# Fused cosformer attention and a GELU layer: the first chunk by halves of heads, and one batch's x turned a block earlier

## The chip, the cores and the metric

One core of a Trainium2 chip runs the whole kernel. The metric is the device time of one execution in microseconds (us), over three runs. A profiled execution of the same kernel gives the trace; its times count from the start of its span. The engines are called PE (matrix products), DVE (vector), ACT (scalar functions), POOL and SP; POOL and SP also issue most transfers (DMA).

## The reference

Eight batches, 8 heads, 576 positions, head size 64. `phi` is ReLU, weighted by a cosine and a sine of the position, so it has 128 features. The attention's result becomes `x` of 4608 tokens by 512, which goes through two matrix products with a GELU between them (2048 wide).

```
q_p = phi(q, cos_w, sin_w)                       # [B,H,S,128]
k_p = phi(k, cos_w, sin_w)
kv  = einsum('bhsf,bhsd->bhfd', k_p, v)          # 128 x 64 per head
z   = sum(k_p, axis=2)                           # 128 per head
num = einsum('bhsf,bhfd->bhsd', q_p, kv)
den = einsum('bhsf,bhf->bhs', q_p, z) + 1e-06
x   = (num / den), heads side by side            # [4608, 512]
h   = x @ w_in;  g = h * sigmoid(1.702 * h);  out = g @ w_out
```

## The kernel before, in words

The work goes batch by batch. The positions of a batch form four chunks of 128 and a tail of 64 (chunk 4). For each batch:

- `trig` (L135) or `trig_q` (L144) makes the weighted ReLU of q and k, in bf16, on DVE, ACT or POOL, two instructions for each `j` (64 positions a head pair).
- `kv_mm` (L202) sums `kv` on PE for pairs of heads `i`, with the row of `z` as a 65th column; `kv_evac` (L210) copies it into `kvs` on DVE. In batch 0 the v tile has no column of ones, and `ksum` (L214) makes `z` by itself, ahead of v's arrival.
- q has to lie features first: in batches 0 and 1 PE transposes it (`qturn_pe`, L167) into PSUM and `qevac` (L174) copies it to `qT` on DVE or ACT; from batch 2 on a DMA does (`qturn_dma`, L187).
- `num_mm` (L226) makes a chunk's numerators of eight heads, with the denominators as each head's 65th column, in a tile of two PSUM banks (four heads in each); `num_div` (L248) adds 1e-6 (`den`), inverts (`inv`) and divides (`xn`) on DVE. `den_early` (L241) makes the denominators by themselves, before the numerators are there.
- x has to lie features first too: in batches 0 and 1 `xturn_mm` (L269) transposes `xn` on PE into columns 264 to 391 of the same PSUM tile, beside the numerators, and `xturn_evac` (L276) copies that to `xT` on ACT; `xturn_dma` (L282) does it by DMA, for the tails in all batches.
- `mm1` (L303) multiplies by `w_in` in sixteen parts `fc` of 128 columns, each over four slices `kc` of 128 features, 512 tokens at a time; `mm1_part` (L291) does so for a range of tokens. `gelu` (L298) follows on ACT. `mm2` (L327) multiplies by `w_out` in ranges of `fc` for each group `t` of 128 tokens, an ACT copy takes the result to `ysb`, and a DMA writes it out. The 64-token tails of all batches go through together at the end.

PSUM has a pool of four one-bank tiles (`pmm`, L46), taken in turn by q's transposes, `den_early`, `mm1` and `mm2`, and a pool of two two-bank tiles (`pat`, L47) for `kv`, the numerators and batch 1's transposes of q. Each new tile waits until the last users of the one before it in that place are done.

The order on each engine is the order in the program; nothing is rescheduled. `idle` (L342) issues products of zeros on PE. At the start (L388 to L440), SP loads k and q of batch 0 in two pieces each, POOL loads v (converted to bf16), the first two parts of `w_in`, and later the rest.

`start_block` (L355) begins the `mm1` of a batch whose x is still being made: the first four `fc` run in parts of 128 tokens, a chunk at a time, between the numerators and the transposes of later chunks. Batches 0 and 1 begin so; batch 1 is called with `opened=True`, because its first two chunks are turned before, during batch 0's last `mm2` groups (L458 to L503). Batches 2 to 7 run all their `mm1` with 512 tokens at a time (L507 on), while q and x of the next batch are turned by DMA.

Of the kernel before, what the change touches and what calls it, by code (L numbers as in the profile page):

```python
# [9 lines left out]
F32 = mybir.dt.float32  # L10
BF16 = mybir.dt.bfloat16
# [8 lines left out]
def kernel(  # L20
# [9 lines left out]
    nc = tc.nc  # L30
# [67 lines left out]
    qn0 = qn.rearrange("p c h f -> p (c h f)")[:, 0:NS * NI * 128].rearrange(  # L98
        "p (j i f) -> p j i f", j=NS, i=NI)
    qT = one.tile([128, H, 640], BF16, name="qT")  # L100
    w_in_sb = [one.tile([128, KC, 512], BF16, name=f"w_in{g}") for g in range(4)]
    w_out_sb = one.tile([128, FC, d_model], BF16, name="w_out_sb")
    nc.gpsimd.memset(vt[:, :, :, 64:66], 1.0)
    nc.gpsimd.memset(qT[:, :, S:640], 0.0)
# [1 line left out]

    win_r = moe_w_in.rearrange("(kc p) f -> p kc f", p=128)
    wout_r = moe_w_out.rearrange("(g p c) d -> p g c d", p=128, c=4)
    w_in_v = [t.rearrange("p k (f c) -> p k c f", c=4) for t in w_in_sb]

    def w_in_of(kc, fc):
        return w_in_v[fc // 4][:, kc, fc % 4, :]

    def load(t, src, b, eng=nc.gpsimd):
        eng.dma_start(out=t, in_=src_of(src, b))
# [5 lines left out]
                            in_=q[b, :, 512:S, :].rearrange("h p d -> p h d"))  # L121

    def load_win(g):
        nc.gpsimd.dma_start(out=w_in_sb[g], in_=win_r[:, :, ts(g, 512)])

    def load_wout(g):
        nc.gpsimd.dma_start(out=w_out_sb[:, ts(g, 4), :], in_=wout_r[:, g])
# [46 lines left out]
    def qevac(c, act=False):  # L174
# [5 lines left out]
        else:  # L180
            nc.vector.tensor_copy(o, i)
# [41 lines left out]

    nums = {}

    def num_mm(c):  # L226
        ps = pat.tile([128, 2, 512], F32, name="at")
        for h in range(H):
            i, hh = divmod(h, 2)
            nc.tensor.matmul(ps[:, h // 4, ds((h % 4) * 65, 65)], qT[:, h, ts(c, 128)],  # L230
                             st["kvs"][:, hh, i, 0:65], start=True, stop=True)
        nums[c] = [ps]

    def inv_of(d):
        den = small.tile([128, 2, 4], F32, name="den")
# [3 lines left out]
        return inv  # L239

    def den_early(c):  # L241
        d = pmm.tile([128, 2, 4], F32, name="mm")
        for h in range(H):
            nc.tensor.matmul(d[:, h // 4, h % 4:h % 4 + 1], qT[:, h, ts(c, 128)],
                             st["kvs"][:, h % 2, h // 2, 64:65], start=True, stop=True)
        return inv_of(d)

    def num_div(c, inv=None):  # L248
        ps = nums[c][0]
        pv = ps[:, :, 0:260].rearrange("p a (h e) -> p a h e", h=4)  # L250
        if inv is None:
            inv = inv_of(pv[:, :, :, 64])
        xn = small.tile([128, 2, 4, 64], BF16, name="xn", bufs=4)
        nc.vector.tensor_tensor(xn, pv[:, :, :, 0:64],  # L254
                                inv.unsqueeze(3).to_broadcast([128, 2, 4, 64]), op=MUL)
        nums[c].append(xn)
# [9 lines left out]
    def x_of(b, c):  # L266
        return xt[:, :, ts(b, 64)] if c == 4 else x[b][:, :, ts(c, 128)]

    def xturn_mm(c):  # L269
        ps, xn = nums[c]  # L270
        xv = xn.rearrange("p a h e -> p (a h e)")
        for kc in range(KC):
            o = ps[:, kc // 2, ds(264 + (kc % 2) * 64, 64)].bitcast(BF16)
            nc.tensor.transpose(o, xv[:, ts(kc, 128)], ident)  # L274

    def xturn_evac(b, c):  # L276
        ps = nums.pop(c)[0]
        i = ps[:, :, 264:392].bitcast(BF16).rearrange("p a (k t) -> p a k t", k=2)
        o = x_of(b, c).rearrange("p (a k) t -> p a k t", a=2)
        nc.scalar.activation(o, i, AF.Copy)  # L280
# [7 lines left out]
    gT = {}  # L288
    hp = {}

    def mm1_part(b, fc, t0, t1):  # L291
        if t0 == 0:
            hp[fc] = pmm.tile([128, MT], F32, name="mm")
        for kc in range(KC):
            nc.tensor.matmul(hp[fc][:, t0:t1], w_in_of(kc, fc), x[b][:, kc, t0:t1],  # L295
                             start=(kc == 0), stop=(kc == KC - 1))
# [58 lines left out]
    def start_block(b, opened=False):  # L355

        if not opened:
            xturn_mm(0)
            xturn_evac(b, 0)
            num_mm(2)  # L360
            num_div(2)
            xturn_mm(1)
            xturn_evac(b, 1)
        def part(c, *fcs):
            for fc in fcs:
                mm1_part(b, fc, c * 128, c * 128 + 128)

        part(0, 0, 1, 2, 3)
        num_mm(3)
        num_div(3)  # L370
        xturn_mm(2)
        xturn_evac(b, 2)
        part(1, 0, 1, 2, 3)
        xturn_mm(3)
        xturn_evac(b, 3)
        num_mm(4)
        num_div(4)
        xturn_dma(b, 4)
        part(2, 0, 1, 2)
        part(3, 0, 1)  # L380
        part(2, 3)
        part(3, 2, 3)
        for fc in range(4):
            gelu(fc)
        mm1(b, 4)
# [25 lines left out]
    idle(2, w)
    qturn_pe(1)
    for j in (4, 5):
        trig(qn0, qf0, j)
    trig(qn0, qf0, 8, eng=nc.gpsimd)
    nc.gpsimd.tensor_copy(gate[0:1, 1:2], vb[0:1, 3, 0:1])
    load_win(2)
    load_win(3)
    kv_mm(0, 2, vb_rhs, 0, 64)
    qturn_pe(2)  # L420
    for j in (6, 7):
        trig(qn0, qf0, j, act=True)
    qevac(0)
    qevac(1)
    qevac(2, act=True)
    inv0 = den_early(0)
    kv_evac(0, 2, 64)
    kv_mm(2, 4, vb_rhs, 0, 64)
    kv_evac(2, 4, 64)
    qturn_pe(3)  # L430
    qevac(3, act=True)
    num_mm(0)
    num_div(0, inv0)
    num_mm(1)
    num_div(1)
    qturn_pe(4)
    qevac(4)
    idle(1)
    x_open(0)
    start_block(0)  # L440


    load(kf, k, 1)
# [15 lines left out]
        mm2(0, t, 0, 4)  # L459
    mm2(0, 0, 4, 8)  # L460
    mm2(0, 1, 4, 8)
    ha = at_homes()
    qturn_pe(0, ha[0])
    qturn_pe(1, ha[1])
    qevac(0)
    qevac(1, act=True)
    mm2(0, 2, 4, 8)
    mm2(0, 3, 4, 8)
    hb = at_homes()
    qturn_pe(2, hb[0])  # L470
    qturn_pe(3, hb[1])
    vcopy(0, 2)
    vcopy(2, 4, act=True)
    qevac(2)
    qevac(3, act=True)
    load_q(2, nc.gpsimd)
    load(kf, k, 2, nc.gpsimd)
    load(vf, v, 2, nc.gpsimd)
    mm2(0, 0, 8, 12)
    mm2(0, 1, 8, 12)  # L480
    hc = at_homes()
    qturn_pe(4, hc[0])
    qevac(4)
    kv_open()
    kv_mm(0, 4, vt_rhs, 0, 65)
    kv_evac(0, 4)
    mm2(0, 2, 8, 12)
    mm2(0, 3, 8, 12)
    num_mm(0)
    num_div(0)  # L490
    num_mm(1)
    num_div(1)
    x_open(1)
    mm2(0, 0, 12, 16)
    mm2(0, 1, 12, 16)
    xturn_mm(0)
    xturn_evac(1, 0)
    mm2(0, 2, 12, 16)
    xturn_mm(1)
    xturn_evac(1, 1)  # L500
    num_mm(2)
    num_div(2)
    mm2(0, 3, 12, 16)  # L503
    start_block(1, opened=True)


    for b in range(1, B):  # L507
        nb = b + 1 if b + 1 < B else None
        f0 = 5 if b == 1 else 0
        for fc in range(f0, FC):  # L510
            if nb is not None and fc == f0:
                for c in range(5):
                    trig_q(c)
                    qturn_dma(c)
                if nb + 1 < B:
                    load_q(nb + 1)
            if nb is not None and fc == f0 + 1:
                for j in range(NS if b > 1 else 5):
                    trig(kr, kf, j)
                vcopy(0, 4 if b > 1 else 2)  # L520
            mm1(b, fc)
            if b == 1 and fc in (7, 9, 11, 13):
                trig(kr, kf, (fc + 3) // 2, act=True)
        if b == 1:
            vcopy(2, 4, act=True)
        if nb is None:
            for fc in range(FC):
                mm1_tails(fc)
            for t in (4, 5, 6, 7):
                mm2(b, t, 0, FC)  # L530
            for t in range(3):
                mm2(b, t, 0, FC)
            mm2(b, 3, 0, FC, 0, 256)
            mm2(b, 3, 0, FC, 256, 512)
            continue
        x_open(nb)
        lag = 1 if b == 1 else 0
        for u in range(8):
            if u == lag:
                kv_open()  # L540
# [40 lines left out]
```

## Time and profile before

| | us |
|---|---|
| median of three runs | 292.51 (292.34 to 292.56) |
| the profiled execution | 292.51 |
| its span, first to last instruction | 290.8 |
| first `mm1` matmul of batch 0 | 16.20 |
| first `mm2` matmul of batch 0 | 31.38 |
| first `mm2` matmul of batch 1 | 65.11 |
| k of batch 0 lands (first, second piece) | 4.2, 6.1 |

A timeline row gives the start, the duration, the engine, the line, the operation with what it writes and reads, and in brackets the idle time of the engine ahead of it with what ended that. Rows of the same kind that follow each other are merged, and their number stands behind `x`. PE's matmuls are pipelined, so a matmul's own duration (0.19 us even for a small one) overlaps with the next one's: for what a matmul adds, look at the distance between starts. In the chain of the last work (shares of the span) PE has 92%, DMA 5%, DVE and POOL 1% each.

### The profile page before, as it was taken

Reading aid. Unit: us, or ns where it says so; the run is one execution under the profiler, and the core shown is the slowest. Engines: PE = TensorE matmul, PEld = TensorE weight load, DVE = VectorE, ACT = ScalarE, POOL = GpSimd, SP = SyncE. Lnnn points to the kernel's source line nnn. Section 1 sums busy time; section 2 is a strip of 40 time slices with the busy share of each in tenths; the row PEclk is TensorE's granted clock in tenths of the full one; section 3 lists DMA queues with packets and bytes.
Section 4 is the critical chain, followed back from the end, with each engine's and each line's share of the span. In section 5 each row is a group of like instructions: output and inputs, shape, how many; then the busy total and the mean of one; then the engine's idle time right before and its main releaser. Section 6 shows DMA issues by size and latency. Waiting matters only on the chain.

```text
span 290.8 us, 5789 instructions
## 1 busy us (share of the span) xinstructions
PE 284.3 (98%) x2330; PEld 154.8 (53%) x2330; DVE 124.1 (43%) x356; ACT 132.9 (46%) x232; POOL 37.8 (13%) x71
## 2 busy tenths in 40 slices
PE   7989999999999999999999999999999999999995
PEld 2775466755555554555455545554555455544444
DVE  4953645842648363826582567156624200000000
ACT  7957654693156214721463136412651167751111
POOL 6650044101210001001100110011000100002000
PEclk9999999999999999999999999999999999999999
DMA  7999999684689958975699469756975400002322
GB/s 250 244 214 287 372 267 363 172 181 128 126 225 306 220 132 276 260 197 145 225 277 227 122 192 335 184 143 152 379 94 74 117 36 3 0 0 44 87 88 72
DMA packets 67771, 52.48 MB, mean 180 GB/s; under 512 B 47969, under 2 KB 57953, under 8 KB 67745
## 3 DMA queue, kind: packets, MB, share of 16 engines
q1 hardware_dynamic: 60320, 32.52, 45.2%
q0 software_dynamic: 7424, 19.60, 23.6%
q8 instruction: 18, 0.29, 0.4%
q14 instruction: 9, 0.07, 0.1%
HBM read 36.70 MB, written 9.44 MB: 159 GB/s over the span
## 4 chain that ended last, share of the span: by engine, by line
PE 92%; DMA 5%; DVE 1%; POOL 1%; issue 0%; ACT 0%; ACTq 0%
PE mm L332 43%; PE mm L295 38%; PE mm L312 5%; DMA w_in<-in_moe_w_in_dram 3%; PE at L230 3%; PE at L207 3%; DMA kf<-in_k_dram 1%; PE at L171 1%; POOL vb L132 1%; DVE xn L254 0%; PE at L274 0%; DVE inv L238 0%; ACT ysb L336 0%; DVE den L236 0%; POOL gate L130 0%
## 5 line engine op out<-in xcount | busy, mean ns | idle before, releaser
L332 PE MATMUL mm<-w_out_sb,g 128*128 128x512 bf16 (+1 forms) x528 | 117.9, 373 | 0.0
L295 PE MATMUL mm<-xT,w_in 128*128 128x512 bf16 (+1 forms) x608 | 112.9, 345 | 0.2 <-DMA w_in<-in_moe_w_in_dram 0.2
L300 ACT ACTIVATE g<-mm 128x512 bf16<-128x512 f32 x128 | 75.1, 598 | 30.4 <-PE mm L295 30.2
L295 PEld LDWEIGHTS <-w_in 128*128 128x128 bf16 x608 | 61.6, 113 | 49.6 <-DMA w_in<-in_moe_w_in_dram 0.3
L332 PEld LDWEIGHTS <-g 128*128 128x128 bf16 x528 | 48.7, 97 | 49.6
L336 ACT ACTIVATE ysb<-mm 128x512 f32<-128x512 f32 (+1 forms) x37 | 21.7, 586 | 109.7 <-PE mm L332 106.7
L340 POOL DMA_DIRECT2D out_dram<-ysb x39 | 21.2, 547 | 205.6 <-ACT ysb L336 203.6
L142 DVE TENSOR_SCALAR kr<-kf,cosw 128x256 bf16<-128x256 f32 x64 | 22.5, 351 | 30.3 <-DMA kf<-in_k_dram 30.3
L254 DVE TENSOR_TENSOR xn<-at,inv 128x512 bf16<-128x512 f32 x40 | 27.7, 691 | 1.7 <-PE at L230 0.4
L142 DVE TENSOR_SCALAR kr<-kf,sinw 128x256 bf16<-128x256 f32 x64 | 22.6, 354 | 0.0
L236 DVE TENSOR_SCALAR den<-at 128x8 f32<-128x8 f32 x39 | 6.5, 166 | 34.4 <-PE at L230 34.4
L230 PEld LDWEIGHTS <-qT 128*128 128x128 bf16 x320 | 14.6, 97 | 8.1 <-issue 0.8
L212 DVE CAST kvs<-at 128x520 bf16<-128x520 f32 (+1 forms) x9 | 5.7, 635 | 28.9 <-PE at L207 28.9
L230 PE MATMUL at<-kvs,qT 128*128 128x65 bf16 x320 | 15.9, 193 | 0.7 <-ACT xT L280 0.7
L155 DVE TENSOR_SCALAR qn<-qf,sinw 128x512 bf16<-128x512 f32 (+1 forms) x30 | 14.4, 480 | 0.0
L155 DVE TENSOR_SCALAR qn<-qf,cosw 128x512 bf16<-128x512 f32 (+1 forms) x30 | 14.3, 476 | 0.0
L312 PE MATMUL mm<-xt,w_in 128*128 128x512 bf16 x64 | 14.0, 379 | 0.0
L332 PE MATMUL mm<-w_out_sb,gl_t 128*128 128x512 bf16 x64 | 14.0, 379 | 0.0
L313 ACT ACTIVATE gl_t<-mm 128x512 bf16<-128x512 f32 x16 | 9.6, 597 | 4.2 <-PE mm L312 4.2
L312 PEld LDWEIGHTS <-w_in 128*128 128x128 bf16 x64 | 7.2, 113 | 6.6
L207 PEld LDWEIGHTS <-kr 64*128 64x128 bf16 x576 | 9.3, 94 | 2.7 <-issue 2.5
L332 PEld LDWEIGHTS <-gl_t 128*128 128x128 bf16 x64 | 6.3, 98 | 7.5
(63 smaller groups left out, 115.4 us busy)
## 6 DMA issues: line engine op xcount, KB each, us to landing
kf<-in_k_dram SPq DMA_DIRECT2D x5, 1152.0 KB, 6.9
vf<-in_v_dram SPq DMA_DIRECT2D x5, 1152.0 KB, 9.6
qf<-in_q_dram SPq DMA_DIRECT2D x5, 1024.0 KB, 6.2
out_dram<-ysb POOLq DMA_DIRECT2D x20, 256.0 KB, 2.8
out_dram<-ysb POOLq DMA_DIRECT2D x19, 128.0 KB, 4.1
kf<-in_k_dram POOLq DMA_DIRECT2D x2, 1152.0 KB, 11.7
vf<-in_v_dram POOLq DMA_DIRECT2D x2, 1152.0 KB, 16.5
w_in<-in_moe_w_in_dram POOLq DMA_DIRECT2D x4, 512.0 KB, 10.2
```

Of the source, the lines that this page charges most:

```text
L142: eng.tensor_scalar(o, i, 0.0, w[:, j:j + 1], op0=MAX, op1=MUL)
L155: nc.vector.tensor_scalar(o, i, 0.0, sc, op0=MAX, op1=MUL)
L207: nc.tensor.matmul(st["kv", i][:, hh, ds(col, n)], kr[r, j, i, :], rhs(r, i, j), start=(j == 0), stop=(j == NS - 1))
L230: nc.tensor.matmul(ps[:, h // 4, ds((h % 4) * 65, 65)], qT[:, h, ts(c, 128)], st["kvs"][:, hh, i, 0:65], start=True, stop=True)
L254: nc.vector.tensor_tensor(xn, pv[:, :, :, 0:64], inv.unsqueeze(3).to_broadcast([128, 2, 4, 64]), op=MUL)
L295: nc.tensor.matmul(hp[fc][:, t0:t1], w_in_of(kc, fc), x[b][:, kc, t0:t1], start=(kc == 0), stop=(kc == KC - 1))
L300: nc.scalar.activation(g, hp.pop(fc), AF.Gelu_apprx_sigmoid)
L312: nc.tensor.matmul(hps, w_in_of(kc, fc), xt[:, kc, :], start=(kc == 0), stop=(kc == KC - 1))
L313: nc.scalar.activation(gl_t[:, fc, :], hps, AF.Gelu_apprx_sigmoid)
L332: nc.tensor.matmul(yp[t, c0][:, c0:c1], w, w_out_sb[:, fc, c0:c1], start=(fc == 0), stop=(fc == FC - 1))
L336: nc.scalar.activation(ysb[:, c0:c1], yp[t, c0][:, c0:c1], AF.Identity)
L340: eng.dma_start(out=dst[:, c0:c1], in_=ysb[p0:p0 + n, c0:c1])
```

## The change

Three things. (1) Batch 0's chunk 0 is handled by halves of heads: its numerators, division, transposes and copies run for heads 0 to 3 as soon as their `kv` is there, and then for heads 4 to 7; the first `mm1` matmuls start with the two slices of features that the first half gives. (2) The first part of `w_in` is loaded as two tiles of two slices each, by two transfers. (3) The order of all engines from the first transposes of q to the first `mm1` of batch 0 is new: `den_early` for chunk 1 too, one `idle` less, and the last 64 positions of q are transposed into the num tile of chunk 2 (`qturn_last`), copied by ACT. In batch 1, `start_block` is gone: all its nums, divisions and turns stand between the `mm2` groups of batch 0, and its `mm1` runs over 512 tokens from `fc` 0. Some copies change engine (q's chunk 2 of batch 1 to ACT, the second half of v to DVE), and the work for batch 2 that was started at `fc` 5 of batch 1 is started at `fc` 0.

```diff
+    w_in0 = [one.tile([128, 2, 512], BF16, name=f"w_in0{u}") for u in "ab"]
...
+        if g == 0:
+            for u in range(2):
+                nc.gpsimd.dma_start(out=w_in0[u], in_=win_r[:, ds(2 * u, 2), 0:512])
...
+    def qturn_last(c_home):
+        for i in range(NI):
+            o = nums[c_home][0][:, i // 2, ds(264 + (i % 2) * 64, 64)].bitcast(BF16)
+            nc.tensor.transpose(o, qn0[:, NS - 1, i, :], ident)
+
+    def qevac_last(c_home):
+        nc.scalar.activation(qT[:, :, ds(512, 64)].rearrange("f (a h) p -> f a h p", a=2),
+                             nums[c_home][0][:, :, 264:392].bitcast(BF16).rearrange(
+                                 "f a (h p) -> f a h p", h=4), AF.Copy)
...
-    def num_mm(c):
-        ps = pat.tile([128, 2, 512], F32, name="at")
-        for h in range(H):
+    def num_mm(c, h0=0, h1=H):
+        if h0 == 0:
+            nums[c] = [pat.tile([128, 2, 512], F32, name="at")]
+        ps = nums[c][0]
+        for h in range(h0, h1):
...
-    def num_div(c, inv=None):
+    def num_div(c, inv=None, a0=0, a1=2):
...
-    def xturn_mm(c):
+    def xturn_mm(c, a0=0, a1=2):
...
-    def xturn_evac(b, c):
-        ps = nums.pop(c)[0]
+    def xturn_evac(b, c, a0=0, a1=2):
+        ps = nums[c][0] if a1 < 2 else nums.pop(c)[0]
...
-    def mm1_part(b, fc, t0, t1):
+    def mm1_part(b, fc, t0, t1, k0=0, k1=KC):
```

The head after the change, from the copy of `z` on:

```
    ksum_evac()
    trig(qn0, qf0, 8, eng=nc.gpsimd)
    nc.gpsimd.tensor_copy(gate[0:1, 1:2], vb[0:1, 3, 0:1])
    load_win(2)
    load_win(3)
    idle(1, w)
    qturn_pe(0)
    for j in (2, 3):
        trig(qn0, qf0, j, act=True)
    trig(qn0, qf0, 4)
    qevac(0)
    trig(qn0, qf0, 5)
    for j in (6, 7):
        trig(qn0, qf0, j, act=True)
    idle(2, w)
    kv_mm(0, 2, vb_rhs, 0, 64)
    qturn_pe(1)
    kv_evac(0, 2, 64)
    qevac(1, act=True)
    inv0 = den_early(0)
    num_mm(0, 0, 4)
    kv_mm(2, 4, vb_rhs, 0, 64)
    num_div(0, inv0, 0, 1)
    kv_evac(2, 4, 64)
    x_open(0)
    xturn_mm(0, 0, 1)
    qturn_pe(2)
    xturn_evac(0, 0, 0, 1)
    inv1 = den_early(1)
    qevac(2, act=True)
    num_mm(0, 4, 8)
    num_mm(1)
    num_div(0, inv0, 1, 2)
    num_div(1, inv1)
    qturn_pe(3)
    for fc in (0, 1):
        mm1_part(0, fc, 0, 128, 0, 2)
    xturn_mm(0, 1, 2)
    xturn_evac(0, 0, 1, 2)
    xturn_mm(1)
    xturn_evac(0, 1)
    qevac(3)
    num_mm(2)
    num_div(2)
    qturn_last(2)
    qevac_last(2)
    for fc in (0, 1):
        mm1_part(0, fc, 0, 128, 2, 4)
    part(0, 2, 3)
    num_mm(3)
    num_div(3)
    part(1, 0)
    xturn_mm(2)
    xturn_evac(0, 2)
    part(1, 1, 2, 3)
    part(2, 0)
    xturn_mm(3)
    xturn_evac(0, 3)
    num_mm(4)
    num_div(4)
    xturn_dma(0, 4)
    part(2, 1, 2)
    part(3, 0, 1)
    part(2, 3)
    part(3, 2, 3)
    for fc in range(4):
        gelu(fc)
    mm1(0, 4)
```

Batch 0's second product after the change, from its first `mm2` groups (fc 0 to 3 of all t, and 4 to 7 of t 0 and 1) on:

```
    mm2(0, 2, 4, 8)
    ha = at_homes()
    qturn_pe(0, ha[0])
    qturn_pe(1, ha[1])
    qevac(0)
    qevac(1, act=True)
    vcopy(0, 2)
    vcopy(2, 4)
    mm2(0, 3, 4, 8)
    hb = at_homes()
    qturn_pe(2, hb[0])
    qturn_pe(3, hb[1])
    qevac(2, act=True)
    qevac(3, act=True)
    ...
    kv_open()
    kv_mm(0, 4, vt_rhs, 0, 65)
    kv_evac(0, 4)
    mm2(0, 0, 8, 12)
    hc = at_homes()
    qturn_pe(4, hc[0])
    qevac(4)
    num_mm(0)
    num_div(0)
    mm2(0, 1, 8, 12)
    num_mm(1)
    num_div(1)
    mm2(0, 2, 8, 12)
    mm2(0, 3, 8, 12)
    x_open(1)
    xturn_mm(0)
    xturn_evac(1, 0)
    mm2(0, 0, 12, 16)
    num_mm(2)
    num_div(2)
    xturn_mm(1)
    xturn_evac(1, 1)
    mm2(0, 1, 12, 16)
    num_mm(3)
    num_div(3)
    xturn_mm(2)
    xturn_evac(1, 2)
    mm2(0, 2, 12, 16)
    num_mm(4)
    num_div(4)
    xturn_mm(3)
    xturn_evac(1, 3)
    xturn_dma(1, 4)
    mm2(0, 3, 12, 16)
```

More of the change, by code (lines that the diff above doesn't have):

```diff
@@ L100 @@
     qT = one.tile([128, H, 640], BF16, name="qT")
-    w_in_sb = [one.tile([128, KC, 512], BF16, name=f"w_in{g}") for g in range(4)]
+    w_in0 = [one.tile([128, 2, 512], BF16, name=f"w_in0{u}") for u in "ab"]
+    w_in_sb = [one.tile([128, KC, 512], BF16, name=f"w_in{g}") for g in range(1, 4)]
     w_out_sb = one.tile([128, FC, d_model], BF16, name="w_out_sb")
@@ L108 @@
     wout_r = moe_w_out.rearrange("(g p c) d -> p g c d", p=128, c=4)
+    w_in0_v = [t.rearrange("p k (f c) -> p k c f", c=4) for t in w_in0]
     w_in_v = [t.rearrange("p k (f c) -> p k c f", c=4) for t in w_in_sb]
     def w_in_of(kc, fc):
-        return w_in_v[fc // 4][:, kc, fc % 4, :]
+        if fc < 4:
+            return w_in0_v[kc // 2][:, kc % 2, fc, :]
+        return w_in_v[fc // 4 - 1][:, kc, fc % 4, :]
     def load(t, src, b, eng=nc.gpsimd):
@@ L123, in load_win @@
     def load_win(g):
-        nc.gpsimd.dma_start(out=w_in_sb[g], in_=win_r[:, :, ts(g, 512)])
+        if g == 0:
+            for u in range(2):
+                nc.gpsimd.dma_start(out=w_in0[u], in_=win_r[:, ds(2 * u, 2), 0:512])
+        else:
+            nc.gpsimd.dma_start(out=w_in_sb[g - 1], in_=win_r[:, :, ts(g, 512)])
     def load_wout(g):
@@ L231, in num_mm @@
                              st["kvs"][:, hh, i, 0:65], start=True, stop=True)
-        nums[c] = [ps]
     def inv_of(d):
@@ L241, in den_early @@
     def den_early(c):
-        d = pmm.tile([128, 2, 4], F32, name="mm")
+        if c == 0:
+            st["den"] = pmm.tile([128, 2, 2, 4], F32, name="mm")
+        d = st["den"][:, c]
         for h in range(H):
@@ L252, in num_div @@
             inv = inv_of(pv[:, :, :, 64])
[L253 to L256, printed above, removed]
+        if a0 == 0:
+            nums[c].append(small.tile([128, 2, 4, 64], BF16, name="xn", bufs=4))
+        nc.vector.tensor_tensor(nums[c][1][:, a0:a1], pv[:, a0:a1, :, 0:64],
+                                inv[:, a0:a1].unsqueeze(3).to_broadcast([128, a1 - a0, 4, 64]), op=MUL)
     x = {}
@@ L267, in x_of @@
         return xt[:, :, ts(b, 64)] if c == 4 else x[b][:, :, ts(c, 128)]
-    def xturn_mm(c):
+    def xturn_mm(c, a0=0, a1=2):
         ps, xn = nums[c]
         xv = xn.rearrange("p a h e -> p (a h e)")
-        for kc in range(KC):
+        for kc in range(2 * a0, 2 * a1):
             o = ps[:, kc // 2, ds(264 + (kc % 2) * 64, 64)].bitcast(BF16)
             nc.tensor.transpose(o, xv[:, ts(kc, 128)], ident)
-    def xturn_evac(b, c):
-        ps = nums.pop(c)[0]
-        i = ps[:, :, 264:392].bitcast(BF16).rearrange("p a (k t) -> p a k t", k=2)
-        o = x_of(b, c).rearrange("p (a k) t -> p a k t", a=2)
+    def xturn_evac(b, c, a0=0, a1=2):
+        ps = nums[c][0] if a1 < 2 else nums.pop(c)[0]
+        i = ps[:, a0:a1, 264:392].bitcast(BF16).rearrange("p a (k t) -> p a k t", k=2)
+        o = x_of(b, c).rearrange("p (a k) t -> p a k t", a=2)[:, a0:a1]
         nc.scalar.activation(o, i, AF.Copy)
@@ L289 @@
     hp = {}
-    def mm1_part(b, fc, t0, t1):
-        if t0 == 0:
+    def mm1_part(b, fc, t0, t1, k0=0, k1=KC):
+        if t0 == 0 and k0 == 0:
             hp[fc] = pmm.tile([128, MT], F32, name="mm")
-        for kc in range(KC):
+        for kc in range(k0, k1):
             nc.tensor.matmul(hp[fc][:, t0:t1], w_in_of(kc, fc), x[b][:, kc, t0:t1],
@@ L353, in vt_rhs @@
         return vt[r, j, i, 0:65]
[L355 to L385, printed above, removed]
     w = idle(12)
@@ L406 @@
     ksum_evac()
+    trig(qn0, qf0, 8, eng=nc.gpsimd)
+    nc.gpsimd.tensor_copy(gate[0:1, 1:2], vb[0:1, 3, 0:1])
+    load_win(2)
+    load_win(3)
     idle(1, w)
@@ L410, with part @@
         trig(qn0, qf0, j, act=True)
[L411 to L420, printed above, removed]
+    trig(qn0, qf0, 4)
+    qevac(0)
+    trig(qn0, qf0, 5)
     for j in (6, 7):
         trig(qn0, qf0, j, act=True)
-    qevac(0)
-    qevac(1)
+    idle(2, w)
+    kv_mm(0, 2, vb_rhs, 0, 64)
+    qturn_pe(1)
+    kv_evac(0, 2, 64)
+    qevac(1, act=True)
+    inv0 = den_early(0)
+    num_mm(0, 0, 4)
+    kv_mm(2, 4, vb_rhs, 0, 64)
+    num_div(0, inv0, 0, 1)
+    kv_evac(2, 4, 64)
+    x_open(0)
+    xturn_mm(0, 0, 1)
+    qturn_pe(2)
+    xturn_evac(0, 0, 0, 1)
+    inv1 = den_early(1)
     qevac(2, act=True)
[L426 to L429, printed above, removed]
+    num_mm(0, 4, 8)
+    num_mm(1)
+    num_div(0, inv0, 1, 2)
+    num_div(1, inv1)
     qturn_pe(3)
[L431 to L440, printed above, removed]
+    for fc in (0, 1):
+        mm1_part(0, fc, 0, 128, 0, 2)
+    xturn_mm(0, 1, 2)
+    xturn_evac(0, 0, 1, 2)
+    xturn_mm(1)
+    xturn_evac(0, 1)
+    qevac(3)
+    num_mm(2)
+    num_div(2)
+    qturn_last(2)
+    qevac_last(2)
+    def part(c, *fcs):
+        for fc in fcs:
+            mm1_part(0, fc, c * 128, c * 128 + 128)
+    for fc in (0, 1):
+        mm1_part(0, fc, 0, 128, 2, 4)
+    part(0, 2, 3)
+    num_mm(3)
+    num_div(3)
+    part(1, 0)
+    xturn_mm(2)
+    xturn_evac(0, 2)
+    part(1, 1, 2, 3)
+    part(2, 0)
+    xturn_mm(3)
+    xturn_evac(0, 3)
+    num_mm(4)
+    num_div(4)
+    xturn_dma(0, 4)
+    part(2, 1, 2)
+    part(3, 0, 1)
+    part(2, 3)
+    part(3, 2, 3)
+    for fc in range(4):
+        gelu(fc)
+    mm1(0, 4)
     load(kf, k, 1)
@@ L461 @@
     mm2(0, 1, 4, 8)
+    mm2(0, 2, 4, 8)
     ha = at_homes()
@@ L466 @@
     qevac(1, act=True)
-    mm2(0, 2, 4, 8)
+    vcopy(0, 2)
+    vcopy(2, 4)
     mm2(0, 3, 4, 8)
@@ L471 @@
     qturn_pe(3, hb[1])
-    vcopy(0, 2)
-    vcopy(2, 4, act=True)
-    qevac(2)
+    qevac(2, act=True)
     qevac(3, act=True)
@@ L478 @@
     load(vf, v, 2, nc.gpsimd)
+    kv_open()
+    kv_mm(0, 4, vt_rhs, 0, 65)
+    kv_evac(0, 4)
     mm2(0, 0, 8, 12)
-    mm2(0, 1, 8, 12)
     hc = at_homes()
@@ L483 @@
     qevac(4)
-    kv_open()
-    kv_mm(0, 4, vt_rhs, 0, 65)
-    kv_evac(0, 4)
+    num_mm(0)
+    num_div(0)
+    mm2(0, 1, 8, 12)
+    num_mm(1)
+    num_div(1)
     mm2(0, 2, 8, 12)
     mm2(0, 3, 8, 12)
[L489 to L492, printed above, removed]
     x_open(1)
-    mm2(0, 0, 12, 16)
-    mm2(0, 1, 12, 16)
     xturn_mm(0)
     xturn_evac(1, 0)
-    mm2(0, 2, 12, 16)
+    mm2(0, 0, 12, 16)
+    num_mm(2)
+    num_div(2)
     xturn_mm(1)
     xturn_evac(1, 1)
-    num_mm(2)
-    num_div(2)
+    mm2(0, 1, 12, 16)
+    num_mm(3)
+    num_div(3)
+    xturn_mm(2)
+    xturn_evac(1, 2)
+    mm2(0, 2, 12, 16)
+    num_mm(4)
+    num_div(4)
+    xturn_mm(3)
+    xturn_evac(1, 3)
+    xturn_dma(1, 4)
     mm2(0, 3, 12, 16)
-    start_block(1, opened=True)
     for b in range(1, B):
         nb = b + 1 if b + 1 < B else None
-        f0 = 5 if b == 1 else 0
-        for fc in range(f0, FC):
-            if nb is not None and fc == f0:
+        for fc in range(FC):
+            if nb is not None and fc == 0:
                 for c in range(5):
@@ L516 @@
                     load_q(nb + 1)
-            if nb is not None and fc == f0 + 1:
+            if nb is not None and fc == 1:
                 for j in range(NS if b > 1 else 5):
```

## The prediction

> **What bounds the kernel.** I read the page first, then PE's timeline, then the chain.
>
> ```profile
> PE 284.3 (98%) x2330; PEld 154.8 (53%) x2330; DVE 124.1 (43%) x356; ACT 132.9 (46%) x232; POOL 37.8 (13%) x71
> PEclk9999999999999999999999999999999999999999
> ```
>
> TensorE is the bound, at full clock throughout. The list of PE's waits holds only four, the longest 1.2 us at the start. The waits between matmuls must be found by arithmetic: where PE's start-to-start distance is longer than the work in it. PE's timeline for block 0, then for block 1:
>
> ```profile
> 14.33 0.40 PE L274 MATMUL at<-ident,xn 128*128 128x128 bf16 x4
> 15.41 0.40 PE L230 MATMUL at<-kvs,qT 128*128 128x65 bf16 x8 [0.69 <-ACT xT L280]
> 15.65 0.39 PE L274 MATMUL at<-ident,xn 128*128 128x128 bf16 x4
> 16.20 1.09 PE L295 MATMUL mm<-xT,w_in 128*128 128x128 bf16 x16 [0.16 <-DMA w_in<-in_moe_w_in_dram]
> ...
> 31.38 5.34 PE L332 MATMUL mm<-w_out_sb,g 128*128 128x512 bf16 x24
> ...
> 51.32 1.06 PE L295 MATMUL mm<-xT,w_in 128*128 128x128 bf16 x16
> 52.48 0.40 PE L274 MATMUL at<-ident,xn 128*128 128x128 bf16 x4
> ...
> 65.11 1.89 PE L332 MATMUL mm<-w_out_sb,g 128*128 128x512 bf16 x8
> ```
>
> The first column is the start, the second the duration. Prices are from start to next start: 0.22 us for a turn (transposes) of four, 0.46 for eight (11.25 to 11.71), 0.24 for eight num matmuls (15.41 to 15.65), 0.64 for 36 kv matmuls (10.61 to 11.25), 0.054 for a matmul of 128 columns and 0.216 for 512 (the chain has 64 of these in 13.81). So four parts of 128 columns cost what one of 512 does. From 65.11 on the chain is PE without a wait, so a shift there passes to the end unchanged.
>
> **Block 1.** From 31.38 to 65.11 are 33.73 us. The work in it: 64 mm2 and 64 mm1 matmuls 27.63, kv 1.20, turns of q 2.0, num 1.2, turns of x 0.88, together 32.9 to 33.0. So about 0.77 us is waiting, most of it around 51 to 53: after num 3 (51.10) the turn of chunk 3 comes at 52.48, though only 0.22 + 0.86 of work lies between. The change spreads nums and turns between mm2 groups and leaves mm1 whole. Each round is then four mm2 matmuls, one num and one turn on PE (0.86 + 0.24 + 0.22 = 1.32 us), a y copy and an x copy on ACT (0.60 + 0.60), and den, inv, xn on DVE (0.17 + 0.20 + 0.69 plus hand-overs, 1.15). PE is the longest in every round, by 0.12 over ACT. Walking it through I find 0.1 us of waits (num 3 and mm1 each some 0.05 behind ACT). **Gain 0.67 us.** Moved beside it: the second half of v goes from ACT (1.16) to DVE (0.91) and chunk 2's copy from DVE (0.69) to ACT (1.02). DVE ends v at about 41.3, when PE is in the first half of its kv matmuls (41.0 to 41.6), which need only v's first half; ACT frees the q tile at 42.7, before PE's 43.1. Bounds: nothing, or 0.3 us if v's second half were late by all of its 0.91. w_out's parts are needed up to 1.4 us earlier, and landed 2 to 4 us before. Batch 2's cosine work, its five SP transposes and batch 3's q loads start some 3 to 4 us earlier on DVE and SP, which PE needs only at 67; POOL's v load of batch 2 waits for the moved copy, 0.6 us later, cover about 8 us.
>
> **Block 0.** I place the new order on PE from the first kv matmul, which waits for v (landed 10.6) as before. An end on DVE or ACT to PE's start takes 0.05, back 0.03 (xn ends 14.27, turn 14.33). Two sizes have no row. A division of half the heads: the copy of 256 columns on DVE took 0.40, the full division 0.69; I take 0.40, bounds 0.17 (den, eight columns) and 0.69. Half an x copy on ACT: 1024 columns took 1.02 and 512 took 0.60, which makes 0.39; bounds 0.20 (one column) and 0.60.
>
> | PE | start | set by |
> |---|---|---|
> | kv of heads 0-3, turn q 1, den 0 | 10.61, 11.25, 11.71 | v; PE |
> | num 0 heads 0-3, kv of heads 4-7 | 11.95, 12.07 | PE |
> | turn x 0, first half | 12.96 | den 12.08, inv, half xn to 12.91 |
> | turn q 2, den 1 | 13.07, 13.53 | PE |
> | num 0 heads 4-7, num 1, turn q 3 | 13.77, 13.89, 14.13 | PE |
> | mm1 fc 0,1, kc 0,1 (4) | 14.59 | PE |
> | turn x 0, second half | 14.81 | PE |
> | turn x 1 | 15.28 | xn 1 to 15.23 |
> | num 2 | 15.56 | half x copy to 15.51 |
> | **last turn of q** | **17.16** | **xn 2 to 17.11** |
> | mm1 kc 2,3; fc 2,3; num 3; part 1 of fc 0 | 17.38, 17.60, 18.03, 18.27 | PE |
> | turn x 2, parts 1 | 18.49, 18.71 | PE |
> | part 2 of fc 0 | 19.57 | x copy to 19.52 |
> | turn x 3, num 4, parts 2 | 19.79, 20.01, 20.25 | PE |
> | parts 3, rest | 20.87 | x copy to 20.82 |
> | mm1 fc 4 | 21.95 | PE |
>
> Before, mm1 of fc 4 started at 31.38 minus 48 matmuls of 0.216, at 21.02. **Loss 0.93 us.** The same by waits: from 10.61 the old order waits about 1.85 us, the new 2.43; it adds eight den matmuls (0.24) and drops an idle one (0.22), and turn q 1 (0.46), which lay in the wait for v, now lies behind it.
>
> The bold row decides. The last turn of q now writes into chunk 2's num tile, in columns beside those that xn 2 divides, and stands behind that division in the program. Does PE wait for it? These rows of ACT and DVE in block 1 tell how two engines at one PSUM tile are treated:
>
> ```profile
> 37.66 0.69 DVE L181 COPY qT<-at 128x1024 bf16<-128x1024 bf16 x1 [0.82 <-PE at L171]
> ...
> 38.38 1.02 ACT L179 ACTIVATE qT<-at 128x1024 bf16<-128x1024 bf16 x1 [0.97 <-DVE qT L181]
> ```
>
> PE's sixteen transposes had ended at 37.62 and ACT was free from 37.41, yet it waited 0.97 us until DVE had copied the other half of the same tile. So accesses of one PSUM tile run one after the other, even in different halves. I take it that PE waits: num 2 ends 15.96, den 0.17, inv 0.20, xn 0.69 with hand-overs end at 17.11, 1.36 us in which PE has nothing, and all of mm1 is queued behind it. (A gap of 0.86 us, 14.55 to 15.41, left the old order's granted clock at full; I take that this one does too.) The Trainium skill, PSUM — Partial Sum Buffer, section "PSUM bank collisions raise a hardware error", is narrower: no two engines may be at one bank and the same partitions at once, reads included. That rule speaks against this change: by it PE waits here too, since the turn writes both banks that xn reads, while the two halves of heads, in two banks, would be free of each other; by the row they are not, but the half copy ends at 13.66 and PE comes at 13.77, so rule and row give +0.26 alike, and the chances below go by the row.
>
> **w_in in two tiles** costs POOL one more issue (0.77 us) ahead of 9.59, where it sat idle for 2.07; without that cover the turn of j 8 would be late, but that is wanted at 17. The first half (256 KB at the 207 GB/s of the stretch from 12 to 16 us) lands near 13.3, the second no later than the old 16.15: wanted at 14.59 and 17.38. In the old order w_in held PE for 0.16 only, so this part gives nearly nothing.
>
> **Sum.** 0.93 − 0.67 = +0.26 us. The profiled execution took 292.51 us (span 290.8), just the median of the runs: 292.51 + 0.26 = **292.8**. What a measurement can tell from no change is about 0.2%, 0.59 us; the forecast lies inside it. Its own range: block 0 from +0.6 to +1.3 (half copies at their bounds, some 0.3), block 1 from −0.75 to −0.45, so 292.3 to 293.3.
>
> **Rivals.**
> - *PE does not wait at the last turn of q*, because only overlapping columns are ordered. Then that row starts at 15.8, the waits behind it come out as 0.05, 0.21 and 0.19, and mm1 of fc 4 starts at about 20.6: block 0 gains 0.4, with block 1's stalls a little larger 0.43: 291.7, faster. Against it stands the row of 0.97 us. Chance 0.13.
> - *Block 1 gives nothing back; slower.* ACT has 0.12 us of slack a round, and the y copy stands ahead of the x copy, for which the next num waits, with only two tiles. From 1.32 us of ACT a round on ACT sets the pace; at 1.5 (each copy 0.15 longer, as ACT's copy of v varied by 0.05 and DVE's by 0.16) four rounds lose 0.7, all of the gain: 293.4. For it: margins of 0.05 in four places of my walk; against: the 0.60 us copies hardly vary. Chance 0.20.
> - *The second half of w_in0 is late.* w_in0 landed 4.16 us after v's second half, of which 512 KB at 207 GB/s explain 2.5; were the excess of 1.6 paid by each half, the second would land at 17.8, 0.4 after it is wanted: 293.2. The next w_in landed 11.3 us after its issue, 1.95 behind the first, so the excess does not add up. Chance 0.07.
> - The forecast: 0.60.
>
> So slower by over 0.2% 0.30 (second rival, part of the third and of the forecast's upper end), faster 0.15, within 0.55. The range reaches to the first rival and over the second: 291.6 to 293.5.
>
> **What would show it.** In PE's timeline: a gap of 1.3 to 1.4 us ahead of the last four transposes of q near 17, ended by xn (right), or none (first rival). mm1's first matmuls before 15 without a wait for w_in. mm1 of fc 4 at 21.9 against 21.0. From block 0's first mm2 to block 1's, 33.1 us instead of 33.73; near 33.7 is the second rival. The forecast is wrong above all if PE passes the last turn of q without that gap.

## The result, and the profile after

| | before | after |
|---|---|---|
| median of seven runs each, us | 292.34 (292.22 to 292.56) | 293.35 (293.19 to 293.51) |
| profiled execution, us | 292.51 | 293.19 |
| its span, us | 290.8 | 291.5 |
| first kv matmul of batch 0 | 10.61 | 10.63 |
| first `mm2` matmul of batch 0 | 31.38 | 32.47 |
| first `mm2` matmul of batch 1 | 65.11 | 65.79 |

The changed kernel is slower by a ratio of 1.0033 (95% interval 1.0023 to 1.0043), 1.0 us. The forecast was 292.8, +0.26 us, and the likeliest verdict "within 0.2%". The time lies inside the widest range stated (291.6 to 293.5), but 0.05 us above the forecast's own (292.3 to 293.3), and the verdict fell on the other side.

The page still shows TensorE as the bound, at full clock:

```profile
PE 282.8 (97%) x2255; PEld 153.4 (53%) x2289; DVE 123.7 (42%) x356; ACT 133.9 (46%) x234; POOL 38.3 (13%) x72
PEclk9999999999999999999999999999999999999999
```

The weight loads are 41 fewer (48 parts of 128 columns less, eight den matmuls more, one idle one less); the other 34 of PE's are missing records. What moved is in PE's timeline of the changed kernel (start, duration, and in brackets the wait with its releaser):

```profile
15.41 0.40 PE L295 MATMUL at<-ident,xn 128*128 128x128 bf16 x4 [0.23 <-DVE xn L276]
15.65 0.40 PE L250 MATMUL at<-kvs,qT 128*128 128x65 bf16 x8
17.27 0.38 PE L194 MATMUL at<-ident,qn 128*128 128x128 bf16 x4 [1.22 <-DVE xn L276]
17.49 0.39 PE L316 MATMUL mm<-xT,w_in0b 128*128 128x128 bf16 x4
...
22.11 10.52 PE L316 MATMUL mm<-xT,w_in 128*128 128x512 bf16 x47
32.47 6.21 PE L353 MATMUL mm<-w_out_sb,g 128*128 128x512 bf16 x27
...
65.79 1.89 PE L353 MATMUL mm<-w_out_sb,g 128*128 128x512 bf16 x7
```

The last turn of q (L194) stands 1.22 us by the bracket, and 17.27 − 15.65 − 0.24 = 1.38 us by starts, behind num 2. DVE's rows of the same stretch are the chain in that wait:

```profile
16.09 0.17 DVE L255 TENSOR_SCALAR den<-at 128x8 f32<-128x8 f32 x1
16.29 0.20 DVE L257 RECIPROCAL inv<-den 128x8 f32<-128x8 f32 x1
16.52 0.69 DVE L276 TENSOR_TENSOR xn<-at,inv 128x512 bf16<-128x512 f32 x1
```

The division ends at 17.21 and PE starts at 17.27. So block 0 ends 1.09 us later than before (32.47 against 31.38), and block 1 takes 33.32 us instead of 33.73.

### The profile page after: what moved, and what is told of

Read it like the earlier page. It is cut to its first block, busy times and chain, and to the rows that moved or that the text cites. A ratio compares the mean times of both kernels' runs of the same rounds, so it can differ in the third digit from the quotient of the medians.

```text
span 291.5 us, 5679 instructions
## 1 busy us (share of the span) xinstructions
PE 282.8 (97%) x2255; PEld 153.4 (53%) x2289; DVE 123.7 (42%) x356; ACT 133.9 (46%) x234; POOL 38.3 (13%) x72
## 4 chain that ended last, share of the span: by engine, by line
PE 91%; DMA 3%; ACT 2%; DVE 1%; issue 1%; ACTq 0%; POOL 0%; DVEq 0%
PE mm L353 42%; PE mm L316 37%; PE mm L333 5%; PE at L250 3%; PE at L225 3%; DMA vb<-in_v_dram 2%; ACT g L321 1%; DMA kf<-in_k_dram 1%; PE at L295 1%; DVE xn L276 1%; PE at L179 0%; ACT qT L187 0%; PE mm L179 0%; DVE qT L189 0%; DVE den L255 0%
## 5 line engine op out<-in xcount | busy, mean ns | idle before, releaser
L353 PE MATMUL mm<-w_out_sb,g 128*128 128x512 bf16 (+1 forms) x506 | 116.7, 372 | 1.3 <-issue 0.2
L316 PE MATMUL mm<-xT,w_in 128*128 128x512 bf16 x377 | 83.8, 379 | 0.4
L316 PEld LDWEIGHTS <-w_in 128*128 128x128 bf16 x384 | 43.4, 113 | 39.2
L276 DVE TENSOR_TENSOR xn<-at,inv 128x512 bf16<-128x512 f32 (+1 forms) x41 | 27.7, 677 | 1.4
L316 PE MATMUL mm<-xT,w_in0b 128*128 128x512 bf16 (+1 forms) x87 | 20.2, 320 | 0.1
L316 PE MATMUL mm<-xT,w_in0a 128*128 128x512 bf16 (+1 forms) x87 | 20.3, 320 | 0.0
L250 PE MATMUL at<-kvs,qT 128*128 128x65 bf16 x320 | 16.2, 193 | 0.0
L316 PEld LDWEIGHTS <-w_in0a 128*128 128x128 bf16 x88 | 9.1, 114 | 6.1
L316 PEld LDWEIGHTS <-w_in0b 128*128 128x128 bf16 x88 | 9.0, 113 | 5.7
```

What stands on the lines that cost most here:

```text
L276: nc.vector.tensor_tensor(nums[c][1][:, a0:a1], pv[:, a0:a1, :, 0:64], inv[:, a0:a1].unsqueeze(3).to_broadcast([128, a1 - a0, 4, 64]), op=MUL)
L353: nc.tensor.matmul(yp[t, c0][:, c0:c1], w, w_out_sb[:, fc, c0:c1], start=(fc == 0), stop=(fc == FC - 1))
```

## The experiments

All ratios are against the kernel before, of runs on the same chip, five rounds (the changed kernel's are those of the table above). Different experiments ran on different chips, where the kernel before had medians of 292.32 to 292.35. "Block 0" is the distance from the first kv matmul of batch 0 to the first `mm2`, which takes out that v lands between 10.6 and 11.0 us from run to run; "block 1" is the distance between the first `mm2` of batches 0 and 1. Both are from one trace each.

| kernel | median us | ratio (95% interval) | block 0 | block 1 |
|---|---|---|---|---|
| before | 292.3 | | 20.77 | 33.73 |
| changed | 293.35 | 1.0033 (1.0023, 1.0043) | 21.84 | 33.32 |
| 1 block 0's part alone | 293.61 | 1.0043 (1.0030, 1.0056) | 21.83 | 33.67 |
| 2 block 1's part alone | 291.88 | 0.9986 (0.9977, 0.9995) | 20.42 | 33.26 |
| 3 last turn in its own tile | 292.54 | 1.0008 (0.9999, 1.0017) | 20.88 | 33.38 |
| 4 w_in's first part in one tile | 293.43 | 1.0038 (1.0026, 1.0051) | 21.84 | 33.32 |
| 5 block 1's kv one group later | 293.04 | 1.0026 (1.0017, 1.0036) | 21.84 | 33.11 |
| 6 old block 0, block 1 as in 5 | 291.67 | 0.9976 (0.9966, 0.9986) | 20.38 | 33.11 |
| 7 as 3, turn of q 1 ahead of kv | 292.10 | 0.9998 (0.9989, 1.0006) | 20.54 | 33.33 |
| 8 as 7, block 1 as in 5 | 291.91 | 0.9990 (0.9981, 0.9998) | 20.92 | 33.11 |
| 9 as 7, chunk 0 not in halves | 292.44 | 1.0000 (0.9992, 1.0009) | 20.85 | 33.32 |
| 10 last turn later in the order | 292.70 | 1.0008 (0.9999, 1.0016) | 21.22 | 33.33 |

**1 and 2: each half of the change alone.** The first takes the head up to `mm1` of `fc` 4 from the changed kernel and everything from batch 0's `mm2` on from the old one; the second the other way round.

> Batch 0's part of the change alone (new head, w_in in two tiles), with the old block 1. Theory A (block 0 loses what its new waits add, block 1 gives part of it back, the two are independent): block 0 lost 1.09 us in the trace of the changed kernel (first mm2 of batch 0 at 32.47 instead of 31.38), so about +1.1 us, 293.4, slower than the changed kernel by 0.4 in the trace. Rival B (block 1 gives nothing back and the loss is elsewhere, since the runs differ by 1.0 and the trace by 0.7): +0.7 to +1.0 as with the whole change.

> Batch 1's part of the change alone, with the old block 0. Theory A: block 1 took 33.32 us instead of 33.73 in the changed kernel, so -0.4 us, 291.9; the wait of about 0.30 us ahead of the kv matmuls, behind ACT's copy of q, shows again. Rival B: no change or slower, because the gain in block 1 was only there since block 0 was late and gave DVE, ACT and the transfers more time.

Measured: 293.61 and 291.88. The two differences, +1.28 and −0.45 us, add up to +0.83, near the whole change's +1.01; +1.28 is more than theory A's +1.1, which was read from a trace of before whose block 0 was slower than usual. Theory A holds: block 0 loses, block 1 gives part of it back, whatever the other does. The wait ahead of the kv matmuls shows again in the trace of the second, with 0.23 us. PE's timeline there shows an old block 0 that is 0.3 us faster than the one my prediction was read from:

```profile
15.70 0.39 PE L274 MATMUL at<-ident,xn 128*128 128x128 bf16 x4
15.93 1.06 PE L295 MATMUL mm<-xT,w_in 128*128 128x128 bf16 x16
...
31.08 6.21 PE L332 MATMUL mm<-w_out_sb,g 128*128 128x512 bf16 x27
...
64.34 1.89 PE L332 MATMUL mm<-w_out_sb,g 128*128 128x512 bf16 x7
```

The first `mm1` follows the turn at once; in the trace of before it started 0.55 us behind the turn, held by w_in (0.33 more than the turn's 0.22). The rows of the DMA issues (KB, us from issue to landing) for w_in's first transfer, before and in this kernel:

```profile
w_in<-in_moe_w_in_dram POOLq DMA_DIRECT2D x1, 512.0 KB, 10.2
```

```profile
w_in<-in_moe_w_in_dram POOLq DMA_DIRECT2D x1, 512.0 KB, 8.6
```

The same transfer took 10.2 us in one execution and 8.6 in another.

**3: the wait at the last turn of q.**

```diff
     qturn_pe(3)
+    q4 = pmm.tile([128, 2, NI, 128], BF16, name="mm")
...
-    qturn_last(2)
-    qevac_last(2)
+    qturn_pe(4, q4)
+    qevac(4, act=True)
```

> The changed kernel with the last 64 positions of q transposed into a tile of their own, at the same place in PE's order; the tile is taken from the pool of four ahead of mm1's first tiles. Theory A (PE waited 1.4 us for the division because turn and division share a PSUM tile): the wait goes, another of about 0.4 comes for the second half of w_in0 (16.2) and one of 0.4 for the copy out of the new tile, and mm1 of fc 4 starts at about 21.2 instead of 22.1: -0.9 us, 292.4. Rival C (PE would have stood still anyway, for w_in or for x): within 0.2 us of the changed kernel.

Measured: 292.54, 0.81 us less than the changed kernel. PE's rows: the turn of four follows num 2 without a wait, and `mm1` of `fc` 4 starts at 21.28.

```profile
15.78 0.40 PE L250 MATMUL at<-kvs,qT 128*128 128x65 bf16 x8
16.01 0.39 PE L179 MATMUL mm<-ident,qn 128*128 128x128 bf16 x4
16.24 0.39 PE L316 MATMUL mm<-xT,w_in0b 128*128 128x128 bf16 x4
...
21.28 10.52 PE L316 MATMUL mm<-xT,w_in 128*128 128x512 bf16 x47
```

The order on PE is the same and only the tile differs, so the wait was for the tile, as theory A says; rival C falls. The wait for w_in's second half, which I expected, did not come in this execution; the one for the copy out of the new tile did, with 0.27 us.

**10: the same wait, hidden by order instead.** The turn stays in the num tile, but `mm1`'s rest of chunk 0 and num 3 go ahead of it:

```diff
-    qturn_last(2)
-    qevac_last(2)
     for fc in (0, 1):
         mm1_part(0, fc, 0, 128, 2, 4)
     part(0, 2, 3)
     num_mm(3)
     num_div(3)
-    part(1, 0)
+    qturn_last(2)
+    qevac_last(2)
+    part(1, 0, 1, 2, 3)
     xturn_mm(2)
     xturn_evac(0, 2)
-    part(1, 1, 2, 3)
-    part(2, 0)
     xturn_mm(3)
     xturn_evac(0, 3)
+    part(2, 0)
```

> The changed kernel with the last turn of q in the num tile of chunk 2 as changed, but behind the rest of chunk 0's mm1 parts and num 3, and the turns of x 2 and 3 behind all parts of chunk 1. Theory A (PE waits for xn 2 whatever stands there; work put in front of the turn hides the wait): the turn stays at about 17.3, the wait shrinks from 1.4 to 0.5, a new one of 0.6 comes ahead of part 2, and mm1 of fc 4 starts near 21.4 instead of 22.1: -0.7 us, 292.65. Rival H (the order behind the turn costs as much as it hides, since x 2's turn waits for the copy of q's last chunk out of the same tile): within 0.2 of the changed kernel, 293.3.

Measured: 292.70 against 292.65 expected. Its PE rows show the wait shrunk and the new one behind it:

```profile
17.10 0.40 PE L250 MATMUL at<-kvs,qT 128*128 128x65 bf16 x8
17.68 0.38 PE L194 MATMUL at<-ident,qn 128*128 128x128 bf16 x4 [0.18 <-DVE xn L276]
...
19.87 0.27 PE L316 MATMUL mm<-xT,w_in0a 128*128 128x128 bf16 x2 [0.46 <-ACT xT L301]
```

**4: w_in in one tile.** `load_win(0)` and `w_in_of` as before the change, all else as changed.

> The changed kernel with the first part of w_in in one tile again, loaded by one transfer. My prediction on record said that the two tiles give nearly nothing: then 293.3 as the changed kernel. Theory D (in the new order the first mm1 matmuls stand ahead of the turns of x, so that w_in0's landing near 16.2 holds all of PE): the matmuls wait from 14.7 to 16.3, everything behind them moves by 1.6 us, 294.9.

Measured: 293.43, as the changed kernel (293.35). Theory D falls, though not for the reason on record: in this execution w_in landed 8.6 us after its issue, at 14.8, and the first `mm1` matmuls came at 14.94, just behind it and 4.05 us behind the first kv matmul, as in the changed kernel.

```profile
14.94 0.39 PE L315 MATMUL mm<-xT,w_in 128*128 128x128 bf16 x4
```

That four of the five runs lie within 293.27 to 293.44 says that a landing near 16.2 is not the rule. What two tiles are worth in an execution in which w_in lands late is left open.

**5 and 6: block 1's kv.**

```diff
-    kv_open()
-    kv_mm(0, 4, vt_rhs, 0, 65)
-    kv_evac(0, 4)
     mm2(0, 0, 8, 12)
+    kv_open()
+    kv_mm(0, 4, vt_rhs, 0, 65)
+    kv_evac(0, 4)
+    mm2(0, 1, 8, 12)
     hc = at_homes()
     qturn_pe(4, hc[0])
     qevac(4)
     num_mm(0)
     num_div(0)
-    mm2(0, 1, 8, 12)
+    mm2(0, 2, 8, 12)
     num_mm(1)
     num_div(1)
-    mm2(0, 2, 8, 12)
     mm2(0, 3, 8, 12)
```

> The changed kernel with batch 1's kv matmuls one mm2 group later (after fc 8 to 11 of t 0, the turn of q's last chunk and num 0 after the group of t 1). Theory A: in the changed kernel PE stood from 41.17 to 41.47 ahead of kv, until ACT had copied q's second chunk out of the PSUM tile that kv takes; 0.86 us of other work in that place hides all of it: -0.3 us, 293.05. Rival E (the wait only moves, to the turn of the last chunk, which takes the other tile, free at 43.36, or to num 0 behind kv's copy): within 0.1 us of the changed kernel.

> The old block 0 with the changed block 1 and its kv matmuls one mm2 group later. Theory A: the gains add, -0.4 and -0.3: 291.6, faster than every kernel so far. Rival E: 291.9 as batch 1's part alone.

The wait in the changed kernel: PE's turns of chunks 2 and 3 start at 40.27 and hold 0.90, but kv starts at 41.47. Rows of PE, DVE and ACT:

```profile
38.51 1.06 PE L179 MATMUL at<-ident,qn 128*128 128x128 bf16 x16
...
40.27 1.06 PE L179 MATMUL at<-ident,qn 128*128 128x128 bf16 x16
41.47 1.26 PE L225 MATMUL at<-vt,kr 64*128 64x65 bf16 x72
```

```profile
39.60 0.69 DVE L189 COPY qT<-at 128x1024 bf16<-128x1024 bf16 x1 [2.18 <-PE at L179]
```

```profile
40.39 1.02 ACT L187 ACTIVATE qT<-at 128x1024 bf16<-128x1024 bf16 x1 [2.38 <-DVE qT L189]
```

DVE's copy of chunk 0 starts when PE has ended both turns (39.57), ACT's copy of chunk 1 when DVE's has ended, and kv starts at 41.47, right behind the end of ACT's at 41.41. With one `mm2` group in between (kernel 5), PE goes on without that wait:

```profile
40.25 1.06 PE L179 MATMUL at<-ident,qn 128*128 128x128 bf16 x16
41.14 1.03 PE L353 MATMUL mm<-w_out_sb,g 128*128 128x512 bf16 x4
42.10 1.26 PE L225 MATMUL at<-vt,kr 64*128 64x65 bf16 x72
```

Measured: 293.04 (0.31 less than the changed kernel, as expected) and 291.67 (0.21 less than kernel 2, where 0.3 was expected; by the traces the block's gain is 0.15 to 0.21, for 0.1 remains ahead of kv). Rival E falls. Kernel 6 is the fastest of all, faster than before by a ratio of 0.9976 (0.9966 to 0.9986).

**7 and 8: the turn of chunk 1.** `qturn_pe(1)` goes ahead of `kv_mm(0, 2, ...)` again, on top of experiment 3; kernel 8 has the `mm2` order of 5 as well.

> The changed kernel with the last turn of q in a tile of its own, and the turn of q's chunk 1 ahead of the first kv matmuls again, as before the change, where it fills the wait for v. Theory A (that turn, 0.46 us, stands on the path behind v): the first kv matmuls start 0.1 later (the turn needs ACT's work up to 10.3), the rest up to 0.4 earlier: about -0.3 us against the kernel with the tile of its own, 292.2. Rival F (the path goes over DVE's copy and division, which wait for kv, so that PE's earlier turn only makes longer waits): 292.5 as that kernel.

> The three repairs of the changed kernel together: last turn of q in a tile of its own, turn of chunk 1 ahead of kv, batch 1's kv one group later. Theory A: 292.5 - 0.3 - 0.3 = 291.9, so the changed kernel's idea is repaired below the old kernel, but not below the old block 0 with the new block 1. Rivals E and F: between 292.2 and 292.5.

Measured: 292.10, 0.44 less than kernel 3, a little more than theory A's 0.3, and 291.91 for all repairs together. (The ratios against before, 0.9998 and 1.0008, put kernel 7's gain at 0.29 us, and the traces' block 0 at 0.34.) Kernel 7's PE rows: the turn ends in the wait for v, and part of the gain goes into a wait for DVE's copy of kv, as rival F said of all of it.

```profile
10.26 0.62 PE L179 MATMUL mm<-ident,qn 128*128 128x128 bf16 x8
10.84 0.71 PE L225 MATMUL at<-vb,kr 64*128 64x64 bf16 x36
...
12.06 0.28 PE L250 MATMUL at<-kvs,qT 128*128 128x65 bf16 x4 [0.23 <-DVE kvs L230]
```

Kernel 8's block 0 took 20.92 in its trace, 0.38 more than kernel 7's with the same order. (This execution took 292.16, 0.25 more than kernel 8's median.) Both traces have a wait without a releaser at the same place, in `mm1` of `fc` 2, longer by 0.38 in kernel 8. Kernel 7's rows, then kernel 8's:

```profile
16.14 0.28 PE L316 MATMUL mm<-xT,w_in0a 128*128 128x128 bf16 x2
16.74 0.27 PE L316 MATMUL mm<-xT,w_in0b 128*128 128x128 bf16 x2 [0.32 <-issue]
```

```profile
16.04 0.28 PE L316 MATMUL mm<-xT,w_in0a 128*128 128x128 bf16 x2
17.01 0.27 PE L316 MATMUL mm<-xT,w_in0b 128*128 128x128 bf16 x2 [0.70 <-issue]
```

No data can explain it, for earlier matmuls had read the same part of `xT` and written the same PSUM tile, and `w_in0b` had been read for `fc` 0. What the traces show is a coincidence with the loading of instructions. In kernels 3, 7, 8 and 10 PE stops behind its 226th weight load, whatever matmul that belongs to (`fc` 2 in three of them, `fc` 3 in kernel 10), and goes on at 16.73, 16.74, 17.01 and 16.99. That is 2.2 to 2.4 us after a 16 KB transfer of instructions starts (14.44, 14.48, 14.66, 14.78). In the changed kernel PE comes to this place only at 17.8, with that transfer started at 14.21, and has no such wait. So the wait is probably for PE's instructions, an argument from these traces that no run tests.

**9: the halves.** Chunk 0's numerators, division, turn and copy for all eight heads at once, on top of 7.

> The changed kernel with two repairs (last turn of q in a tile of its own, turn of chunk 1 ahead of kv; 292.1) and without the halves: numerators, division, turn and copy of chunk 0 for all eight heads at once, mm1 from its first matmul with all four slices. Theory A (by walking the rows, num 3 would start at 17.2 instead of 17.07, since PE stands for DVE's divisions either way): +0.1 us, 292.2, not to be told from the kernel with halves. Rival G (the halves are what brings mm1 forward): mm1's first 16 matmuls start at 16.1 instead of 14.5, and half a microsecond or more is lost: 292.6 or above.

Measured: 292.44 (292.15 to 292.99) against 292.10 (292.00 to 292.88) with halves. By the traces, from the first kv matmul to `mm1` of `fc` 4, it is 10.49 against 10.18 us. So these traces and medians give the halves some 0.3 us, between theory A's 0.1 and rival G's 0.5. The runs do not show it beyond their noise: their ranges overlap, and the ratios against before, 0.9998 and 1.0000, differ by 0.06 us only, within their intervals.

## Why the prediction was right in its mechanisms and short in its size

Point by point, by its own steps.

- **The last turn of q: right.** On record 17.16, measured 17.27, with the gap of 1.38 where 1.36 was forecast, ended by xn. Experiments 3 and 10 show that it is the tile, and that it costs 0.8 us. The first rival (no wait) falls. The Trainium skill, PSUM — Partial Sum Buffer, section "PSUM bank collisions raise a hardware error", says that two engines must not be at one bank and the same partitions at once. The turn writes the banks that xn reads, and the gap of 1.38 us fits that. Whether the kernel waits for the whole tile or for these banks, no run here tells apart; nor was the turn tried ahead of the division in the program.
- **The table of block 0: right to 0.16 us.** `mm1` of `fc` 4 was due at 21.95 and came at 22.11. The first 0.14 arises at one row: the half turn of x 0 came at 13.10, not 12.96, because the half division started 0.11 behind the end of inv instead of 0.03, and took 0.02 longer (0.42, where I took 0.40):

```profile
12.31 0.20 DVE L257 RECIPROCAL inv<-den 128x8 f32<-128x8 f32 x1
12.62 0.42 DVE L276 TENSOR_TENSOR xn<-at,inv 128x256 bf16<-128x256 f32 x1
```

The delay is 0.09 at num 2, 0.11 at the last turn, and grows to 0.16 behind it, so part of it is small differences in the prices. The half x copy took 0.38 for 0.39. Why the division started late is not shown.
- **Block 1's gain: mis-sized, 0.41 for 0.67.** "ACT frees the q tile" was worked out for the second tile; for the first I let DVE copy chunk 0 as soon as its own turn was done. The rows I had quoted said otherwise: DVE's copy started at 37.66, right behind the end of both turns at 37.62, and I read in them only that ACT waits for DVE. The three steps in a row (PE, DVE, ACT) at one tile make the 0.30 us ahead of kv, and experiment 5 takes most of it away (0.1 is left). The same kind of wait stood in the old block 1 already, 0.18 us by starts, behind ACT's copy out of the second tile, which ended at 42.15:

```profile
41.13 1.02 ACT L179 ACTIVATE qT<-at 128x1024 bf16<-128x1024 bf16 x1 [0.67 <-DVE qT L181]
```

```profile
42.20 1.26 PE L207 MATMUL at<-vt,kr 64*128 64x65 bf16 x72
```

The second rival (ACT too slow in each round) falls: num 2 to num 4 wait at most 0.1. Its time, 293.4, is nevertheless what was measured, for other reasons: from the total alone one would have picked the wrong cause.
- **w_in: read too small.** I took w_in's hold on the old order as the 0.16 us of the bracket. By starts it was 0.33 (turn at 15.65, 0.22, `mm1` at 16.20), my own rule for all other waits. The second reckoning of the loss, by waits, could have shown it: 2.43 − 1.85 + 0.24 − 0.22 + 0.46 makes 1.06, not 0.93. By starts the old order waits about 1.97 us, and with that the sum comes out. And w_in's hold was a feature of that execution, not of the kernel: in the traces of kernels 2 and 6, with the same old block 0, that block takes 20.42 and 20.38 instead of 20.77. So against these executions the new block 0 loses 1.07 + 0.35, not 0.93.
- **The third rival** (second half of w_in0 late) half happened: in the trace of the changed kernel it landed 9.5 us after its issue, at 16.2, with the first half at 7.3 us. It was wanted at 17.49, so it cost nothing.

The sum: forecast 0.26, plus 0.16 in block 0, 0.26 in block 1 and 0.35 for the base execution, makes 1.03; measured 1.01 by medians. The last term is the least sure. The two profiled executions differ by 0.68 (0.26 + 0.16 + 0.26). The rest, 0.33, is that the one of before took 0.17 more than its median and the changed one 0.16 less; that w_in's landing accounts for it is argued from the block 0 of 20.4 in kernels 2 and 6, and not shown. All three errors went the same way, and that the time still lies inside the widest range is owed to the room left there for the rivals.

The change's own aims: the halves bring 0.3 by the traces, the new order of block 1 0.4, two tiles for w_in nothing that these runs show. What takes it back is one transposition in a borrowed tile (0.8), and a turn moved out of the wait for v (0.3 to 0.4). These terms make +0.4 to +0.5 of the +1.0. The rest fits the other reordering of block 0, which no run takes apart: without the halves and with both repairs (kernel 9) block 0 still takes 20.85 us, against 20.4 in kernels 2 and 6.

## What to carry to other kernels

Spare columns of a PSUM tile were not a free place here: PE's write to them waited until DVE was done with the other columns. So borrow a tile only behind work that hides its last reader, or take one of your own. Measure every wait from start to start, also those with a bracket. And when the base is one execution, ask of each transfer that ends a wait whether it always lands then: the traces of kernels 2 and 6 show the same stretch 0.35 to 0.39 us shorter, more than the whole forecast.

## What the runs showed of the hardware that I had not expected

- The landing of a 512 KB transfer to w_in on POOL's queue comes at two times in four traces: 8.5 to 8.6 us after its issue in kernels 2, 4 and 6, 10.2 in the trace of before, with the queue ahead of it the same. The times of the old kernel do not show two groups: they lie without a gap from 292.12 to 292.76, with four more from 293.11 to 293.19. An instruction transfer of 16 KB runs near 14 us in each trace, close to the end of w_in's; that it is the cause was not tested. Its start alone does not decide: it is 14.21 in the changed kernel, where w_in's second half landed after 9.5 us, and 14.20 in kernel 5, where that took 7.9.
- Two engines' copies out of different halves of one PSUM tile run one after the other in this kernel, and the first also waits for PE's writes into the other half (37.62 to 37.66 before; 39.57 to 39.60 after). Whether the chip needs these waits, no run shows.
